# Unit-step transposes, a new order for the last stage's first two steps, and an earlier first load of h

## The chip, the cores and the metric

The kernel runs on one core of a Trainium2 chip. The metric is the device time of one execution in microseconds (us); before the change the median of three runs is 2382.28 us (2378.8 to 2383.4). The core has TensorE (PE in the profile, its weight loads PEld), VectorE (DVE), ScalarE (ACT), GpSimd (POOL), and SyncE (SP), whose queue issues nearly all DMA transfers. Each engine works through its own list of instructions in order and waits on semaphores of the others.

## The reference

A transformer block on 2048 tokens of width 1024, all in float32:

```python
xn = _layernorm(x)
q, k, v = split(xn @ wqkv)                 # 32 heads of 32
pq, pk = q @ w_phi, k @ w_phi              # per head
phi = concat(softmax(p), softmax(-p))      # per head, for q and for k: 64 features
kv, z = phi_k^T v, sum(phi_k)              # sums over all tokens
o = (phi_q kv) / (phi_q z + 1e-6)
s = o.reshape(S, D) @ wo
h = silu(xn @ w1) * (xn @ w3)              # 3584 wide
return x + s * silu(h @ w2)
```

## The kernel before

Every float32 product is made of three passes on split operands: `split(hi, lo, src)` writes a rounded copy on ScalarE (line 93) and the remainder on VectorE (line 94); TensorE then adds hi·hi, hi·lo and lo·hi. The large products are cut into 2 x 2 blocks and done as seven products with sums of blocks as operands. The seven operands of x are named A11, A12, S2, S1, S3, S4, A22 (`ANAMES`), those of the weights B11 to T4.

**Stage order.** The first stage computes h and stores it in HBM (`h_d`), with x's operands (`xo_d`) and the weights' operands prepared on the side. The second does keys and values, in two passes over eight pairs of token tiles, and then a third pass, the queries (`c == 2`): for each pair `i`, `seven` does seven products of twelve matmuls (line 679) into banks b, a, b, c, b, c, b. Bank b of a pair is one bank: A11's result is copied out of it by ScalarE (`k0`, line 798), then S2 is added into it, copied out (`d0`, line 811), and so on. The spikes (maximum, minimum, subtraction, exponential) follow on VectorE, GpSimd and ScalarE (lines 741 to 746) and go to HBM as `e_d`. The third stage is the product of h with w2 (line 1078), 56 steps of seven products; its operands come from `load_h`, `a_first` and `a_second`. The last stage applies the feature sums and the output projection.

**Loads of the queries.** `reload(i)` takes seven tiles of a ring of eleven (`quad`) and loads x's operands of the next pair at the start of each pair. h's first tile, of the same ring, is loaded by `load_h(0, 0)` in the middle of pair 6; `a_first(0, 0)` in pair 7 splits it.

**Who sets the order.** In the queries the lists of SP and TensorE are as written; those of ScalarE, VectorE and GpSimd are ordered by a planner that has costs for every instruction and fills an engine's idle time with work that it takes to be ready. In the last stage all five lists are as written (`in_order`).

**The last stage.** Tokens are taken in eight steps `b` of two tiles (`SETS[b]`). For a step:

- `load_e(b, c)` loads the exponentials `es` (SP); partition r of a group of 32 and the index u stand for token 4r + u.
- `weigh(b, c)` multiplies them by z, four instructions on GpSimd (line 1005); `add_up(b, c)` sums them per head, four on VectorE (line 1013); `factors(b)` makes the two factors of a head from the sums, seven on VectorE (lines 1022 to 1028); `weights(b)` scales es by them, two on VectorE and two on GpSimd (line 1035).
- `swap(b, c)` transposes blocks of 32 x 32, four instructions on VectorE (line 1042), into `ets`. It writes them so that tokens stand in their own order, 4r + u: each transposed row is written with a step of four floats.
- `heads_out(po)` multiplies with kv on TensorE (128 small matmuls, line 1052) into four banks `po`.
- `operand(t, po)` splits tile t's part of po into the operand `oT` of the projection (lines 93, 94 again).
- `half_out(oT, a, c)` is one projection product of 24 matmuls (line 1205) for tile a and output half c, into one of three banks (`pm`).
- `result(m, p)` multiplies product m with the gate on VectorE (line 1224), which frees the bank, adds x on GpSimd (line 1225), stores the output and loads the gate and x of product m + 3 into one of four `gx` buffers.

A step's TensorE work is: product 0, product 1, the head matmuls for the next step, product 2, product 3 (in step 0 the head matmuls stand behind product 2). Step 0 prepares steps 1 and 2, later steps a little further ahead.

Of the kernel before, what the change touches and what calls it, by code (L numbers as in the profile page):

```python
# [8 lines left out]
F = mybir.dt.float32  # L9
# [8 lines left out]
P = 128  # L18
# [10 lines left out]
def tile_kernel(ctx: ExitStack, tc: tile.TileContext, x, wkT, wqT, wv, wphi, wo, w1, w3, w2, out):  # L29
    nc = tc.nc  # L30
# [33 lines left out]
    ANAMES, BNAMES = [n for _, n, _ in ORDER], [n for _, _, n in ORDER]  # L64
# [26 lines left out]
    def split(hi, lo, src, by=None):  # L91

        nc.scalar.copy(hi, src)  # L93
        (by or nc.vector).tensor_sub(lo, src, hi.bitcast(F))  # L94
# [199 lines left out]
    for j in range(4):  # L294
        sl = slice(32 * j, 32 * j + 32)
# [260 lines left out]
    def operand(k, n):  # L556

        r = raw_of(k)
        src = {"B11": r["B11"], "B21": r["B21"], "T2": wk[4], "T1": r["B11"], "T3": r["B12"], "B22": r["B22"], "T4": r["B21"]}[n]
        bos[k, n] = quad("bo")  # L560
        split(bos[k, n][:, 0], bos[k, n][:, 1], src.rearrange("p (k n) -> p k n", n=P))
# [305 lines left out]
    def load_h(kb, i):  # L867
        hq = quad("hr", F)
        nc.sync.dma_start(hq.rearrange("p b k t -> p (b k t)"),
                          h_d[i // 4][kb][i % 4].rearrange("p b h k t -> p (b h k t)"))  # L870
        return hq
# [44 lines left out]
    for c in range(3):  # L916
        wbn = {}
        if c == 2:
            in_order(ENG.SP, ENG.PE)
            close("spare")  # L920
            bpa = pool("ra", 1, side="right")
        for i in range(len(pairs)):
            nxt, end = {}, i + 1 == len(pairs)

            def steps():
                for j in range(7):
                    if c == 0 and 4 <= 7 * i + j < 40:
                        split_wo(7 * i + j - 4)
                    if j == 0:
                        if i + 2 == len(pairs) and c < 2:  # L930
                            for m in range(2):
                                wbn.update(fetch(c + 3, m))
                        if not (end and c == 2):
                            nxt.update(reload((i + 1) % len(pairs)))
                        if c == 2 and i in (1, 2):
                            load_b(0, i - 1)
                    if c == 2 and end and j in (2, 3):
                        load_b(0, j)
                    for todo in (later, later_s):
                        if todo:  # L940
                            todo.pop(0)()

                    if end and c < 2:
                        if j < 4 or (j == 4 and c == 0):
                            wbn.update(fetch(c + 3, j + 2))
                        if j == 6 and c == 1:
                            wbn.update(fetch(c + 3, 6))
                    if c == 2 and (i, j) == (6, 4):
                        ahead[0, 0] = load_h(0, 0)
                    if c == 2 and (i, j) == (7, 1):  # L950
                        ready.append(a_first(0, 0))
                    if c == 2 and (i, j) == (7, 4):
                        ready.append(a_second(*ready[0]))
                    if c == 2 and (i, j) == (7, 5):
                        ahead[0, 1] = load_h(0, 1)
                    yield

            pend = (queries if c == 2 else heads)(i, xo, wb, steps(), pend)
            xo = nxt
        wb = wbn  # L960
# [38 lines left out]
    def weigh(b, c):  # L999

        z = zb[:, c].unsqueeze(1).to_broadcast([P, 2, 256])
        for t in range(2):
            for u in range(2):
                ez[b, t, c, u] = work.tile([P, 2, 256], F, name="ez", tag="w")
                nc.gpsimd.tensor_mul(ez[b, t, c, u], es[b, t, c][:, 2 * u:2 * u + 2], z)  # L1005

    def add_up(b, c):

        if c == 0:
            zs[b] = small.tile([P, 4, 2, 2, 8], F, name="zs", tag="sums")  # L1010
        for t in range(2):
            for u in range(2):
                nc.vector.tensor_reduce(zs[b][:, 2 * u:2 * u + 2, t, c], ez.pop((b, t, c, u)).rearrange("p u (h f) -> p u h f", f=DH),  # L1013
                                        axis=AX.X, op=OP.add)

    def factors(b):

        s4 = s_in[:, :, b // 4, b % 4].rearrange("p u (h s) -> p u h s", s=2)
        z4 = zs.pop(b).rearrange("p u t c (h s) -> p u (t c h) s", s=2)
        by[b] = work.tile([P, 4, 2, 2, 8], F, name="by", tag="h1", bufs=2)  # L1020
        b4 = by[b].rearrange("p u t c (h s) -> p u (t c h) s", s=2)
        nc.vector.reciprocal(rho, s4[:, :, :, 1])
        nc.vector.tensor_mul(rho, s4[:, :, :, 0], rho)
        nc.vector.tensor_mul(den, z4[:, :, :, 1], rho)
        nc.vector.tensor_add(den, z4[:, :, :, 0], den)
        nc.vector.reciprocal(b4[:, :, :, 0], den)
        nc.vector.tensor_mul(b4[:, :, :, 1], b4[:, :, :, 0], rho)
        nc.vector.tensor_copy(by0, by[b][:, :, :, 0])
# [8 lines left out]
    def swap(b, c):  # L1037

        for q in range(2):
            ets[c, q] = accp.tile([P, 4, 2, 32, 4], F, name="et", tag=f"acc{4 + 2 * c + q}")  # L1040
            for t in range(2):
                nc.vector.transpose(ets[c, q][:, :, t].rearrange("p k r u -> p u k r"),  # L1042
                                    es[b, t, c][:, :, 128 * q:128 * q + 128].rearrange("p u (k f) -> p u k f", f=DH))

    def heads_out(po):

        for c in range(2):
            for s in range(2):
                for j in range(4):
                    for a in range(4):  # L1050
                        sl = slice(32 * a, 32 * a + 32)
                        nc.tensor.matmul(po[a][32 * j:32 * j + 32, 256 * c:256 * c + 256], kvt[sl, c, j, s],  # L1052
                                         ets[c, j // 2][sl, 2 * (j % 2) + s].rearrange("p t r u -> p (t r u)"),
                                         start=c == 0 and s == 0, stop=c == 1 and s == 1, skip_group_check=True)

    def operand(t, po):

        two = [quad("oT") for _ in range(2)]
        for m, (a, src) in enumerate(po):
            o = two[a // 2].rearrange("p u (b c) t -> p u b c t", c=2)  # L1060
            if src.shape[1] == 2:
                split(o[:, 0], o[:, 1], src.rearrange("p b (c t) -> p b c t", c=2)[:, :, :, P * t:P * t + P])
            else:
                split(o[:, 0, a % 2], o[:, 1, a % 2], src.rearrange("p (c t) -> p c t", c=2)[:, :, P * t:P * t + P])
        return two

    def product(kb, i, bank, r, ao, b, an, bn):
# [162 lines left out]
    def weights(b):  # L1230

        scale(b, 0, nc.vector)
        scale(b, 1, nc.gpsimd)
# [7 lines left out]
    for b in range(NB):  # L1241
        p0 = half_out(oT, 0, 0)
        if b == 0:
            add_up(1, 1)
            factors(1)
            weights(1)
            swap(1, 0)
            load_e(3, 0)
            swap(1, 1)
            load_e(3, 1)  # L1250
            weigh(2, 0)
        else:
            result(4 * b - 1, last)
            if b + 1 < NB:
                swap(b + 1, 1)
                load_e(b + 3, 1)
            if b + 2 < NB:
                weigh(b + 2, 1)
                add_up(b + 2, 1)
                factors(b + 2)  # L1260
        p1 = half_out(oT, 0, 1)
        result(4 * b, p0)
        if 0 < b < NB - 1:
            heads_out([po[a // 2][:, a % 2] for a in range(4)])
        p2 = half_out(oT, 1, 0)
        result(4 * b + 1, p1)
        if b == 0:
            weigh(2, 1)
            add_up(2, 0)
            heads_out([po[a // 2][:, a % 2] for a in range(4)])  # L1270
            nxt = [operand(t, [(0, po[0]), (2, po[1])]) for t in range(2)]
            add_up(2, 1)
            factors(2)
            weights(2)
        else:
            if b + 2 < NB:
                weights(b + 2)
            if b + 1 < NB:
                nxt = [operand(t, [(0, po[0]), (2, po[1])]) for t in range(2)]
        if b + 2 < NB:  # L1280
            swap(b + 2, 0)
            load_e(b + 4, 0)
        if b + 3 < NB:
            weigh(b + 3, 0)
        last = half_out(oT, 1, 1)
        result(4 * b + 2, p2)
        if b + 3 < NB:
            add_up(b + 3, 0)
        oT = nxt
# [41 lines left out]
```

## Time and profile before

| what | value |
|---|---|
| median of three runs | 2382.28 us (2378.8 to 2383.4) |
| the profiled execution: time, span | 2379.08 us, 2377.0 us |
| granted TensorE clock, mean | 0.997 |
| busy, share of the span: DVE, ACT, POOL | 75%, 36%, 32% |
| queries (third pass) | about 1488 to 1635 us |
| product with w2 | about 1635 to 2172 us |
| last stage | about 2172 to 2377 us |

A row of the profile's timeline gives start, length, engine, line, operation, what it writes and reads with the shape, how many instructions of a kind are merged, and in brackets how long the engine stood idle before it and what ended that. Consecutive instructions overlap a little (the next starts before the last has drained), so the spacing from start to start is what an engine spends. A row of the waits gives engine, line and what it waited for: us in total, times, longest. A row by stretches of time gives span, busy time (and count) of PE, PEld, DVE, ACT, POOL, then the granted clock, the transfers' share and GB/s.

### The profile page before, as it was taken

The page shows a single profiled execution, that of the slowest core. Times are in us where ns is not written, and L with a number is a line of the kernel's source. Part 1 is how long each engine was busy: PE and PEld are TensorE (multiplying, and loading weights), DVE is VectorE, ACT ScalarE, POOL GpSimd, SP SyncE. Part 2 cuts the span into 40 slices and gives each one's busy share as a digit, 9 for nine tenths or more (in the row PEclk, how much of TensorE's full clock was granted, in tenths as well). Part 3 has the DMA queues.
Part 4 walks back from the last instruction along what each step waited for, and adds up shares of the span by engine and source line. Part 5 has one row for each costly group of instructions (what it writes and reads, how often), then busy time and mean ns, then how long its engine had stood idle before and what let it go on. Part 6 is the DMA issues. An engine that isn't in the chain of part 4 may idle for free. (4 is left out here: it accounts for less than half of the span.)

```text
span 2377.0 us, 35821 instructions
## 1 busy us (share of the span) xinstructions
PE 2341.7 (99%) x13298; PEld 1927.9 (81%) x13298; DVE 1771.6 (75%) x2511; ACT 856.9 (36%) x1506; POOL 758.4 (32%) x569
## 2 busy tenths in 40 slices
PE   6999999999999999999999999999999999999999
PEld 5888888888788888888888788887888888887777
DVE  8567798775688878885576665787678788888993
ACT  6445554443354444453221211234423222242010
POOL 1233555452455555652000000230011111114872
PEclk9999999999999999999999999999999999999999
DMA  7667789877877787776998867998444453277653
GB/s 263 198 217 235 233 288 315 285 251 224 258 272 263 247 280 274 262 270 224 362 347 337 321 221 281 348 352 294 154 145 158 177 185 138 94 274 293 222 190 121
DMA packets 319406, 586.83 MB, mean 247 GB/s; under 512 B 25600, under 2 KB 158208, under 8 KB 316544
## 3 DMA queue, kind: packets, MB, share of 16 engines
q1 hardware_dynamic: 304448, 569.87, 69.7%
q10 hardware_dynamic: 14784, 14.68, 1.8%
q8 instruction: 105, 1.72, 0.3%
q14 instruction: 69, 0.57, 0.1%
HBM read 379.19 MB, written 205.79 MB: 246 GB/s over the span
## 5 line engine op out<-in xcount | busy, mean ns | idle before, releaser
L94 DVE TENSOR_TENSOR bo<-rw,bo 128x512 fp32r<-128x512 f32 x336 | 310.7, 925 | 150.9 <-ACT bo L93 148.5
L1088 POOL TENSOR_TENSOR acc<-acc,u 128x512 f32<-128x512 f32 x48 | 63.5, 1323 | 450.9 <-ACT u L1087 427.9
L93 ACT CAST bo<-rw 128x512 fp32r<-128x512 f32 x336 | 201.1, 617 | 3.9 <-DMA w_d0T<-w2o 2.0
L1078 PE MATMUL bankb<-bo,as 128*128 128x512 f32 x816 | 200.7, 389 | 0.0
L1078 PEld LDWEIGHTS bankb<-bo,as 128*128 128x128 f32 x816 | 153.2, 188 | 31.8
L1205 PE MATMUL pm<-wos,oT 128*128 128x512 f32 x720 | 168.8, 393 | 3.6 <-DVE gx L1224 3.6
L627 PE MATMUL bankb<-op0A,bo 128*128 128x512 f32 x672 | 164.0, 391 | 0.3 <-DVE op0A L94 0.3
L1205 PEld LDWEIGHTS pm<-wos,oT 128*128 128x128 f32 x720 | 135.6, 189 | 35.1 <-DVE gx L1224 4.0
L627 PE MATMUL bankb<-op0S,bo 128*128 128x512 f32 x672 | 163.5, 392 | 0.0
L627 PE MATMUL bankc<-op0S,bo 128*128 128x512 f32 x672 | 163.0, 391 | 0.0
L627 PE MATMUL bankc<-op1S,bo 128*128 128x512 f32 x672 | 161.5, 389 | 0.9 <-ACT bo L93 0.9
L627 PE MATMUL bankb<-op1S,bo 128*128 128x512 f32 x672 | 161.6, 389 | 0.8 <-ACT h L569 0.8
L627 PE MATMUL bankb<-op1A,bo 128*128 128x512 f32 x672 | 161.4, 389 | 0.0
L627 PEld LDWEIGHTS bankc<-op1S,bo 128*128 128x128 f32 x672 | 126.0, 188 | 27.5 <-ACT bo L93 1.3
L627 PEld LDWEIGHTS bankb<-op1S,bo 128*128 128x128 f32 x672 | 126.0, 188 | 27.4 <-ACT h L569 1.2
L627 PEld LDWEIGHTS bankb<-op1A,bo 128*128 128x128 f32 x672 | 126.1, 188 | 26.2
L627 PEld LDWEIGHTS bankb<-op0A,bo 128*128 128x128 f32 x672 | 125.4, 188 | 25.9 <-DVE op0A L94 0.5
L627 PEld LDWEIGHTS bankb<-op0S,bo 128*128 128x128 f32 x672 | 125.6, 188 | 25.7
L627 PEld LDWEIGHTS bankc<-op0S,bo 128*128 128x128 f32 x672 | 125.5, 188 | 25.7
L1078 PE MATMUL bankc<-bo,as 128*128 128x512 f32 x576 | 146.2, 389 | 0.0
L1078 PEld LDWEIGHTS bankc<-bo,as 128*128 128x128 f32 x576 | 108.1, 188 | 22.5
L129 POOL TENSOR_TENSOR rw<-rw 128x512 f32<-128x512 f32 x56 | 82.8, 1479 | 135.5 <-DMA rw<-in_w 104.3
(246 smaller groups left out, 4726.1 us busy)
## 6 DMA issues: line engine op xcount, KB each, us to landing
rw<-in_w SPq DMA_DIRECT2D x224, 256.0 KB, 3.4
hr<-h_d SPq DMA_DIRECT2D x56, 512.0 KB, 4.1
xoS<-xo_d0S SPq DMA_DIRECT2D x48, 512.0 KB, 8.7
xoS<-xo_d1S SPq DMA_DIRECT2D x48, 512.0 KB, 7.1
xoA<-xo_d0A SPq DMA_DIRECT2D x36, 512.0 KB, 7.2
xoA<-xo_d1A SPq DMA_DIRECT2D x36, 512.0 KB, 6.1
e<-e_d SPq DMA_DIRECT2D x32, 512.0 KB, 6.2
h_d<-h SPq DMA_DIRECT2D x56, 256.0 KB, 3.9
```

What stands on the lines that cost most here:

```text
L93: nc.scalar.copy(hi, src)
L94: (by or nc.vector).tensor_sub(lo, src, hi.bitcast(F))
L129: nc.gpsimd.tensor_sub(b12, b22, b12)
L627: nc.tensor.matmul(bank, bt[:, w, kk], aos[tb][an][:, u, kk], start=an in ("A11", "A12", "S1") and n == 0, stop=LAST[b] == an and n == 11, ...
L1078: nc.tensor.matmul(bank[b], t[:, u, pos + k], bos[kb, bn, k][:, w], start=first and n == 0, stop=LAST[b] == an and n == 5, skip_group_chec ...
L1088: nc.gpsimd.tensor_add(c, c, u)
L1205: nc.tensor.matmul(p, oT[a][k // 4][:, u, k % 4], wos[c, 4 * (k % 2) + k // 2][:, w], start=n == 0, stop=n == 23)
```

## The change

It has four parts. `swap` writes a transposed row with steps of one float, so that the tokens stand in the order (u, r); `heads_out` keeps that order, and `operand` restores the tokens' order when it reads `po`, with one split for each of the two column halves instead of one for both. Step 0 of the last stage has its work in another order: the sums and weighings of step 2 move ahead of the first two results, the head matmuls come directly behind product 2, each operand is split by itself, the result of product 2 comes ahead of the second operand and of the transposes, and both swaps of step 2 are done in step 0. Step 1 starts with the weighing of step 3 and the result of product 3, and does its sums and factors behind the head matmuls. In the queries, `load_h(0, 0)` is issued after the third of the last seven loads of x's operands, at the start of pair 6, instead of in its middle.

```diff
@@ queries, inside steps() @@
-                        if not (end and c == 2):
+                        if c == 2 and i == 6:
+                            nxt.update(reload(7, ANAMES[:3]))
+                            ahead[0, 0] = load_h(0, 0)
+                            nxt.update(reload(7, ANAMES[3:]))
+                        elif not (end and c == 2):
                             nxt.update(reload((i + 1) % len(pairs)))
...
-                    if c == 2 and (i, j) == (6, 4):
-                        ahead[0, 0] = load_h(0, 0)
@@ swap @@
-            ets[c, q] = accp.tile([P, 4, 2, 32, 4], F, name="et", tag=f"acc{4 + 2 * c + q}")
+            ets[c, q] = accp.tile([P, 4, 2, 4, 32], F, name="et", tag=f"acc{4 + 2 * c + q}")
             for t in range(2):
-                nc.vector.transpose(ets[c, q][:, :, t].rearrange("p k r u -> p u k r"),
+                nc.vector.transpose(ets[c, q][:, :, t].rearrange("p k u r -> p u k r"),
@@ heads_out @@
-                                         ets[c, j // 2][sl, 2 * (j % 2) + s].rearrange("p t r u -> p (t r u)"),
+                                         ets[c, j // 2][sl, 2 * (j % 2) + s].rearrange("p t u r -> p (t u r)"),
@@ operand @@
-        for m, (a, src) in enumerate(po):
-            o = two[a // 2].rearrange("p u (b c) t -> p u b c t", c=2)
+        for a, src in po:
+            o = two[a // 2].rearrange("p v (b c) (r u) -> p v b c r u", c=2, u=4)
             if src.shape[1] == 2:
-                split(o[:, 0], o[:, 1], src.rearrange("p b (c t) -> p b c t", c=2)[:, :, :, P * t:P * t + P])
+                src = src.rearrange("p b (c t u r) -> p b c t r u", c=2, t=2, u=4)
+                for c in range(2):
+                    split(o[:, 0, :, c], o[:, 1, :, c], src[:, :, c, t])
             else:
-                split(o[:, 0, a % 2], o[:, 1, a % 2], src.rearrange("p (c t) -> p c t", c=2)[:, :, P * t:P * t + P])
+                src = src.rearrange("p (c t u r) -> p c t r u", c=2, t=2, u=4)
+                split(o[:, 0, a % 2], o[:, 1, a % 2], src[:, :, t])
@@ last stage, loop over b @@
             weigh(2, 0)
+            add_up(2, 0)
+            weigh(2, 1)
+        elif b == 1:
+            weigh(3, 1)
+            result(3, last)
         else:
             result(4 * b - 1, last)
...
         result(4 * b + 1, p1)
-        if b == 0:
-            weigh(2, 1)
-            add_up(2, 0)
-            heads_out([po[a // 2][:, a % 2] for a in range(4)])
-            nxt = [operand(t, [(0, po[0]), (2, po[1])]) for t in range(2)]
-            add_up(2, 1)
-            factors(2)
-            weights(2)
+        if b < 2:
+            if b == 0:
+                heads_out([po[a // 2][:, a % 2] for a in range(4)])
+            add_up(b + 2, 1)
+            nxt = [operand(0, [(0, po[0]), (2, po[1])])]
+            factors(b + 2)
+            weights(b + 2)
+            if b == 0:
+                result(2, p2)
+            nxt.append(operand(1, [(0, po[0]), (2, po[1])]))
...
         if b + 2 < NB:
-            swap(b + 2, 0)
-            load_e(b + 4, 0)
+            for c in range(2 if b == 0 else 1):
+                swap(b + 2, c)
+                load_e(b + 4, c)
...
         last = half_out(oT, 1, 1)
-        result(4 * b + 2, p2)
+        if b:
+            result(4 * b + 2, p2)
```

## The prediction

> **What bounds it.** Read first the busy shares, then TensorE's waits, then its timeline, then the other engines around each gap.
>
> ```profile
> PE 2341.7 (99%) x13298; PEld 1927.9 (81%) x13298; DVE 1771.6 (75%) x2511; ACT 856.9 (36%) x1506; POOL 758.4 (32%) x569
> ...
> PE pm L1205 <- DVE gx L1224: 3.6, 1, 3.6
> PE bankb L679 <- ACT k L798: 2.2, 1, 2.2
> PE bankb L1078 <- DVE acc L1090: 1.0, 1, 1.0
> ...
> 1614.11 2.88 PE L679 MATMUL banka<-op4B,xoA 128*128 128x512 f32 x12
> 1619.15 4.60 PE L679 MATMUL bankb<-op4T,xoS 128*128 128x512 f32 x12 [2.17 <-ACT k L798]
> 2188.87 2.75 PE L1052 MATMUL po<-et,kvt 32*32 32x256 f32 x128
> 2197.13 5.60 PE L1205 MATMUL pm<-wos,oT 128*128 128x512 f32 x24
> 2206.35 6.68 PE L1205 MATMUL pm<-wos,oT 128*128 128x512 f32 x21 [3.62 <-DVE gx L1224]
> ```
>
> TensorE is busy 99% of the span: other engines' time counts only where it makes TensorE wait. From the queries on there are two waits of over 1 us, and each costs more than its idle time. After 2.17 us idle, twelve matmuls took 4.60 us where the twelve before took 2.88: 1.72 more. After 3.62 us, 21 took 6.68 us; at the spacing of the row before (24 in 5.60, so about 0.227 each and 0.16 for the last to drain) they take 4.93: 1.75 more. So the wait at 1619 costs 3.89 us and the one at 2206 costs 5.37. Their sum, 9.26 us, is about all that reordering can win here.
>
> ```profile
> 1620.00:1640.00 20.00, 20.00 (x83) 16.35 (x82) 18.16 (x28) 7.96 (x12) 3.15 (x3) 0.92 0.99 346
> ```
>
> This row of 20 us holds the span, the busy time of five engines, the granted clock, and the transfers' share: the clock is 0.92 right behind the shorter gap, so its 1.72 us is a slowed clock. [...]
>
> **The first wait.** In the queries' seventh pair ScalarE, whose order the planner writes, reached h's first cast early and stood there:
>
> ```profile
> 1592.25 0.86 SPq L526 DMA_DIRECT2D xoS<-xo_d1S  x2
> 1595.26 3.04 SPq L526 DMA_DIRECT2D xoS<-xo_d1S  x2
> 1603.78 0.32 SPq L526 DMA_DIRECT2D xoA<-xo_d1A  x1
> 1604.19 0.38 SPq L869 DMA_DIRECT2D hr<-h_d  x1
> DMA to landing us min/median/max: 7.4/8.8/9.9
> ...
> 1595.17 1.06 ACT L746 ACTIVATE eq<-eq 128x1024 f32<-128x1024 f32 x1 [3.06 <-POOL eq L744]
> 1596.67 0.59 ACT L798 COPY k<-bankb 128x512 f32<-128x512 f32 x1 [0.44 <-ACT eq L746]
> 1600.71 0.59 ACT L811 COPY d<-bankb 128x512 f32<-128x512 f32 x1 [0.93 <-PE bankb L679]
> 1611.49 0.62 ACT L93 CAST af<-hr 128x512 fp32r<-128x512 f32 x1 [6.03 <-DMA hr<-h_d]
> 1617.57 1.06 ACT L746 ACTIVATE eq<-eq 128x1024 f32<-128x1024 f32 x1 [3.97 <-POOL eq L744]
> 1618.53 0.57 ACT L798 COPY k<-bankb 128x512 f32<-128x512 f32 x1
> ...
> 1612.15 0.69 DVE L94 TENSOR_TENSOR af<-hr,af 128x512 fp32r<-128x512 f32 x1 [3.33 <-ACT af L93]
> ```
>
> hr is issued at 1604.19, lands about 1611.5, and ScalarE (6.03 us) and VectorE (3.33 us) wait for it. Behind VectorE's stands d (L823), then its maxima, GpSimd's subtraction, the exponential at 1617.57, and behind that the copy of A11's bank, which frees the bank for S2 on TensorE.
>
> The change issues hr fourth of eight loads. That place is now the second of the pair at 1592.25, about 1592.7. Landing 8.8 us later (the xoS median, the row under the SP rows), hr is there at 1601.5, ten us sooner. SP does not change its count: S1, S3, S4 and A22 each move one place, to 1595.3, about 1598, 1603.8 and 1604.2. With the longest landing, 9.9, the last is there at 1614.1; none of the four is multiplied before 1619. The ring of eleven operand tiles hands out as many tiles, so hr's earlier hold costs nothing I can find.
>
> Unknown is where the planner now puts the cast. In this trace it stands where ScalarE was idle soon after the issue. If it stands behind the copy at 1600.71, hr has landed: the whole 3.89 us go. If between the copies of 1596.67 and 1600.71, ScalarE waits until 1601.5, casts twice (0.5 each), perhaps runs one exponential (1.0), and copies by 1603.1 to 1604.1; TensorE wants that bank at about 1603.4: 0 to 0.8 us lost. If ahead of 1596.67, see the second rival. I take the full 3.89, since each next wait (the copy then due at 1614.3 for S2 at 1617) has its work done.
>
> **The second wait, at 2206.** A product's bank (three of them) is freed by `result`; the second step's second product takes the first step's third bank, whose result stood last in VectorE's list:
>
> ```profile
> 2171.90 1.41 DVE L94 TENSOR_TENSOR oT<-po,oT 128x256 fp32r<-128x256 f32 x4
> 2175.27 0.56 DVE L1022 RECIPROCAL stat<-s_in 128x64 f32<-128x64 f32 x1
> 2177.76 2.35 DVE L1035 TENSOR_TENSOR e<-e,stat 128x1024 f32<-128x1024 f32 x2
> 2180.03 7.52 DVE L1042 STREAM_TRANSPOSE et<-e 128x512 f32<-128x512 f32 x8
> 2187.38 1.28 DVE L1224 TENSOR_TENSOR gx<-pm,gx 128x512 f32<-128x512 f32 x2
> 2188.57 2.46 DVE L1013 TENSOR_REDUCE zs<-ez 128x16 f32<-128x512 f32 x4
> 2192.25 2.63 DVE L94 TENSOR_TENSOR oT<-po,oT 128x512 fp32r<-128x512 f32 x4 [1.22 <-ACT oT L93]
> 2194.80 2.46 DVE L1013 TENSOR_REDUCE zs<-ez 128x16 f32<-128x512 f32 x4
> ...
> 2205.61 0.69 DVE L1224 TENSOR_TENSOR gx<-pm,gx 128x512 f32<-128x512 f32 x1
> ...
> 2181.35 5.07 POOL L1005 TENSOR_TENSOR ez<-e,zb 128x512 f32<-128x512 f32 x4
> 2188.20 2.52 POOL L1225 TENSOR_TENSOR gx<-gx 128x512 f32<-128x512 f32 x2 [1.78 <-issue]
> ```
>
> *Spacings.* From start to start: a transpose 0.92 (7.35 for 8), a reduction 0.62, factors 2.5, two scalings 2.27, a result 0.6, an oT subtraction 0.64 whole and 0.33 half.
>
> *Transposes.* They now write unit steps instead of every fourth float. Bounds: 0.92 (writing in shorter steps shouldn't lose) and 0.62, the reduction of equal size. *Operands.* The order of tokens is now restored where oT is read from PSUM, in steps of 32 floats, and the four whole pieces per step become eight halves on ScalarE and on VectorE. Bounds per half: 0.33, and 0.92, as if half a piece cost a whole stepped transpose. I take the transpose at 0.62 and charge the halves the same extra per element (0.30 over 512, so 0.15): 0.48. ScalarE's halves are covered: it is busy 2.25 us of a turn of 24.66 (the row under "Later turns").
>
> [...]
>
> *VectorE's list by these prices.* Eight first halves cost 8 x 0.15 = 1.2 more: factors start at 2176.5, scalings end 2181.2, eight transposes 2186.2 (the head matmuls want them at 2188.9). GpSimd's four weighings end 2187.7, so the moved sums end 2188.3 and two results 2189.5; the fourth product wants the first bank at 2191.6. GpSimd's next four, now ahead of its two result additions, end 2192.7 (so the first two results are stored about 2 us later, and the loads behind those stores on SP's queue too; their gx is used only by results after 2208). Sums 2193.3, first operand 2195.3 (wanted 2197.0), factors 2197.8, scalings 2200.0, and the third result at **2200.6, wanted at 2202.6**: the wait is gone with 2.0 to spare. Then second operand 2202.5, eight transposes 2207.5 (wanted 2208.0 and, for the second half, 2209.3), four sums 2210.0, fourth result 2210.6, wanted at 2210.7. That last is what is late next, with no margin: 0 to 0.5 us. With transposes still at 0.92 and halves at 0.33 the same list gives 2200.2 for the third result and 2211.9 for the fourth: 1.2 lost, 4.2 of 5.37 won.
>
> *Later turns.*
>
> ```profile
> 2241.06:2265.72 24.66, 24.66 (x225) 19.74 (x225) 23.39 (x39) 2.25 (x4) 18.88 (x14) 1.00 0.67 230
> ```
>
> A turn lasts 24.66 us, all TensorE. VectorE's spacings in it: 7.35 transposes, 4.9 sums, 2.5, 2.3, 2.55 oT, 2.4 results, 22.0 in all; after, 8 x 0.62 and 8 x 0.48 for the first and the fifth: 20.9. So the earlier start (5.4) is kept to the end; results, head matmuls and loads are as far ahead of need as now. The last product's tail is untouched.
>
> **Sum.** 3.89 + 5.37 = 9.3 off this execution: 2379.08 us (span 2377.0) to 2369.8. It lies 3.2 below the median of the three runs (2382.28, from 2378.8 to 2383.4), so the median goes to **2373.0**, 0.39% faster. A difference within 0.2% (4.8 us) is about what a measurement of this kernel can't tell from none.
>
> **Rivals.** *One: stepped PSUM reads make VectorE the bound, and it ends slower.* Place: the halves on L94. A turn without transposes and oT is 22.0 - 7.35 - 2.55 = 12.1; with transposes at 0.92 it fills TensorE's 24.66 when a half costs 0.65 us [(24.66 - 12.1 - 7.35)/8], with 0.62 when it costs 0.95 [(24.66 - 12.1 - 4.96)/8]. At 0.92 and unimproved transposes a turn is 12.1 + 7.35 + 7.36 = 26.8: 2.1 over, six turns, 13 us, and some 8 in the first two turns; less the 9.3: about 2394. For it: no row with such a read. Against: the 16-byte step of the transposes costs at most 0.30 on 512. Chance 0.06.
>
> *Two: the wait on hr moves instead of going.* The cast ahead of the copy at 1596.67: hr at 1601.5, two casts, an exponential and its store issue (1.4), the copy: 1604.6, where S2 starts now at 1597.9: 6.7 and 1.7 of clock, 8.4 against 3.9. Total 9.3 - 8.4 = 0.9 gained: 2381.4. For it: ScalarE idles 3.06 us before 1595.17 and took the cast early once. Against: the load would be under 3 us old there. With the wait merely kept as large as now, 2376.9. Chance of either 0.24.
>
> *Three: the last stage gives half or less* (unchanged transposes with halves over 0.5, so that the fourth result and the head matmuls wait), the first wait gone: 2376 to 2378.4. Chance 0.12. *Four: neither pays,* 2382: 0.06.
>
> **Chances and range.** Both waits gone 0.52, at 2372 to 2374.5. Rival two splits: half of its 0.24 ends just beyond 0.2%, half within. Rival three within for two thirds. Faster 0.52 + 0.12 + 0.04 = 0.68, same 0.24, slower 0.08. The range takes in the two cases above 2376 and, below, the lowest run minus all waits of the list, 2378.8 - 9.3 - 1.0 = 2368.5: 2368 to 2382. Own range of the likeliest: 2370 to 2376.
>
> **What would show it.** No wait of TensorE at L679 for ScalarE's k copy and a granted clock of 1.00 after 1600; no cast of hr waiting there. No gap at pm near 2206, and the third result near 2200. Transposes about 0.6 to 0.75 apart, oT subtractions x8 a turn at 0.4 to 0.5. Wrong would make it: a wait of the first casts in front of 1600, halves of 0.65 or more, or a new gap before the second step's third product, near 2211.

## The result, and the profile after

The changed kernel takes 2366.73 us (median of six runs, 2363.33 to 2367.77) against 2378.81 us for the kernel before (six runs, 2376.16 to 2383.4): a ratio of 0.9950 with a 95% interval of 0.9939 to 0.9962, so 0.5% faster. The forecast was 9.3 us less than a median of 2382.28, a ratio of 0.9961, and 2373.0 us with a range of 2368 to 2382. The direction and the two named waits were right; the size was too small and the time lies 1.3 us below the range. The reasons follow below.

The busy shares, from the changed kernel's page:

```profile
PE 2337.4 (99%) x13298; PEld 1925.0 (81%) x13298; DVE 1753.2 (74%) x2539; ACT 859.2 (36%) x1534; POOL 760.5 (32%) x569
```

All of its TensorE waits behind the start-up, from its list of waits (us in total, times, longest):

```profile
PE bankc L627 <- ACT bo L93: 1.0, 1, 1.0
PE pkv L665 <- DVE ev L711: 0.9, 1, 0.9
PE pkv L839 <- DVE zs L838: 0.8, 1, 0.8
PE bankc L679 <- ACT d L818: 0.3, 1, 0.3
```

All three waits that the prediction quoted are gone: ScalarE's copy (2.2 us), VectorE's addition in the product with w2 (1.0) and the result (3.6). None took their place.

**The queries.** Timeline row of TensorE in the changed kernel:

```profile
1616.58 2.88 PE L679 MATMUL bankb<-op4T,xoS 128*128 128x512 f32 x12
```

SP's timeline row of the load of h:

```profile
1592.46 0.39 SPq L869 DMA_DIRECT2D hr<-h_d  x1
```

ScalarE's timeline, the first cast of h and the copy of A11's bank:

```profile
1605.89 0.62 ACT L93 CAST af<-hr 128x512 fp32r<-128x512 f32 x1 [0.68 <-PE bankb L679]
1615.34 0.57 ACT L798 COPY k<-bankb 128x512 f32<-128x512 f32 x1
```

And the row by stretches (span, busy time of PE, PEld, DVE, ACT, POOL, then clock, transfers' share, GB/s):

```profile
1600.00:1640.00 40.00, 40.00 (x178) 33.09 (x177) 35.25 (x53) 16.80 (x24) 6.31 (x6) 1.00 0.92 312
```

S2 starts without a wait, takes the undisturbed 2.88 us, and the clock is 1.00 where it was 0.92. h is issued at 1592.46 (forecast 1592.7) and lands 10.3 us later, at about 1602.8 (forecast 8.8 us later, 1601.5). Its cast runs at 1605.89 and no longer waits for h but for TensorE: the cast writes into a tile of the same ring of eleven, and that tile is free only when a product that reads it ends. In ScalarE's list the cast stands where it stood before, behind the copy at line 818 (1604.88 before, 1604.63 now). The copy that held TensorE runs at 1615.34, 1.2 us ahead of S2.

**The last stage.** VectorE's timeline in the changed kernel:

```profile
2174.15 4.86 DVE L1044 STREAM_TRANSPOSE et<-e 128x512 f32<-128x512 f32 x8
2178.93 2.42 DVE L1015 TENSOR_REDUCE zs<-ez 128x16 f32<-128x512 f32 x4
...
2186.16 0.42 DVE L94 TENSOR_TENSOR oT<-po,oT 128x256 fp32r<-128x256 f32 x1
2187.02 0.76 DVE L94 TENSOR_TENSOR oT<-po,oT 128x256 fp32r<-128x256 f32 x2 [0.44 <-ACT oT L93]
2188.22 0.42 DVE L94 TENSOR_TENSOR oT<-po,oT 128x256 fp32r<-128x256 f32 x1 [0.44 <-ACT oT L93]
2188.56 0.55 DVE L1024 RECIPROCAL stat<-s_in 128x64 f32<-128x64 f32 x1
...
2193.31 0.68 DVE L1229 TENSOR_TENSOR gx<-pm,gx 128x512 f32<-128x512 f32 x1
...
2203.41 1.88 DVE L1229 TENSOR_TENSOR gx<-pm,gx 128x512 f32<-128x512 f32 x3
```

And TensorE's:

```profile
2182.99 2.76 PE L1054 MATMUL po<-et,kvt 32*32 32x256 f32 x128
...
2191.25 10.36 PE L1210 MATMUL pm<-wos,oT 128*128 128x512 f32 x45
...
2204.91 10.49 PE L1210 MATMUL pm<-wos,oT 128*128 128x512 f32 x45
```

Everything here lies 5.88 us earlier than before (head matmuls at 2182.99 for 2188.87). The third result starts at 2193.31 and, at 0.6 us for a result, is done at 2193.9; TensorE wants it at 2196.7, 24 matmuls behind 2191.25: 2.8 us to spare where there were 3.6 us of wait. The fourth, first of the three at 2203.41, is done at 2204.0, and the product that takes its bank starts at 2204.91. Eight transposes take 4.78 us from start to start (2174.15 to 2178.93), 0.60 each.

TensorE's start times at fixed points tell where the 11.1 us between the two profiled spans (2377.0 and 2365.9) came from:

| point | before | after | earlier by |
|---|---|---|---|
| A11 of the queries' pair 6 | 1592.35 | 1592.10 | 0.25 |
| first product with w2 | 1634.50 | 1630.17 | 4.33 |
| last bank a of that stage | 2158.03 | 2152.43 | 5.60 |
| first projection product | 2172.46 | 2166.58 | 5.88 |
| head matmuls of step 1 | 2213.64 | 2202.22 | 11.42 |

So the queries gave 4.1 us (3.9 forecast), the last stage 5.5 (5.4 forecast), and **the product with w2 gave 1.3, and the head matmuls at its end 0.3, that the sum did not hold**. The first 0.25 us were there before the change could act, and of the 11.4 at the last row the two spans keep 11.1.

### The profile page after: what moved, and what is told of

Same layout as the page of the kernel before. It is cut to its first block, busy times and chain, and to the rows that moved or that the text cites. A ratio compares the mean times of both kernels' runs of the same rounds, so it can differ in the third digit from the quotient of the medians.

```text
span 2365.9 us, 35878 instructions
## 1 busy us (share of the span) xinstructions
PE 2337.4 (99%) x13298; PEld 1925.0 (81%) x13298; DVE 1753.2 (74%) x2539; ACT 859.2 (36%) x1534; POOL 760.5 (32%) x569
## 3 DMA queue, kind: packets, MB, share of 16 engines
q8 instruction: 105, 1.72, 0.3%
## 4 chain that ended last, share of the span: by engine, by line
PE 95%; DMA 2%; DVE 2%; SPq 1%; issue 1%; ACT 0%; POOL 0%; ACTq 0%; POOLq 0%; DVEq 0%
PE bankb L627 25%; PE bankb L1083 13%; PE bankc L627 12%; PE bankb L679 11%; PE pm L1210 7%; PE bankc L1083 6%; PE banka L627 6%; PE bankc L679 5%; PE banka L1083 3%; PE banka L679 3%; PE po L1054 1%; PE pkv L665 1%; PE pw L248 1%; SPq L166 0%; PE pt L219 0%
## 5 line engine op out<-in xcount | busy, mean ns | idle before, releaser
L1095 DVE TENSOR_TENSOR acc<-bankb,acc 128x512 f32<-128x512 f32 x152 | 104.3, 686 | 30.8 <-PE bankb L1083 26.6
```

Source lines behind the costliest of these rows:

```text
L1095: nc.vector.tensor_add(c, pb, c)
```

## Experiments

The executions also differ in the first stage, which none of the edits touches: the last wait of the list above (ScalarE's d, early in the queries) ends anywhere from 1506.58 to 1511.12 us in the eleven profiles. So beside the times stands TensorE's time from that matmul's start to the start of the kernel's last three matmuls (on the tile `late`):

| kernel | us, from first to last | ratio of times to before (95%) |
|---|---|---|
| before | 861.13 | |
| changed | 850.01 | 0.9950 (0.9939 to 0.9962) |
| load alone | 857.96 | 0.9979 (0.9971 to 0.9988) |
| all but the load | 854.49 | 0.9973 (0.9963 to 0.9983) |
| layout alone | 865.12 | 0.9998 (0.9989 to 1.0007) |
| all but the layout | 852.82 | 0.9957 (0.9944 to 0.9971) |
| load sixth | 849.88 | 0.9955 (0.9940 to 0.9970) |
| first swap stepped | 850.91 | 0.9960 (0.9946 to 0.9975) |
| halves in turn | 850.03 | 0.9950 (0.9935 to 0.9965) |
| one result moved | 863.03 | 1.0006 (0.9997 to 1.0015) |
| one swap moved back | 851.87 | 0.9952 (0.9938 to 0.9965) |

The two rows of TensorE's timeline that bound it, in before:

```profile
1510.62 3.01 PE L679 MATMUL bankc<-op4B,xoS 128*128 128x512 f32 x12 [0.32 <-ACT d L818]
2371.75 0.84 PE L1205 MATMUL pm<-late,oT 128*128 128x512 f32 x3
```

And in the changed kernel:

```profile
1510.36 3.01 PE L679 MATMUL bankc<-op4B,xoS 128*128 128x512 f32 x12 [0.32 <-ACT d L818]
2360.37 0.84 PE L1210 MATMUL pm<-late,oT 128*128 128x512 f32 x3
```

### The load alone, and all but the load

The first is the kernel before with only this edit, the second the changed kernel without it:

```diff
-                        if not (end and c == 2):
+                        if c == 2 and i == 6:
+                            nxt.update(reload(7, ANAMES[:3]))
+                            ahead[0, 0] = load_h(0, 0)
+                            nxt.update(reload(7, ANAMES[3:]))
+                        elif not (end and c == 2):
...
-                    if c == 2 and (i, j) == (6, 4):
-                        ahead[0, 0] = load_h(0, 0)
```

> The kernel before with h's first load moved ahead of the last four operand loads, nothing else. Theory: each of three waits of TensorE has one cause of its own, and the load is that of the wait at 1619 only. Then 2.17 us of idle time and its slowed restart (1.72) are gone, about 4 us; the 1.0 us wait at 2156 and the 3.6 us wait at 2206 stay, with a 1.2 to 1.8 us slower restart behind the last: 4 us faster than before, 0.17%. Rival A (the load also moves the short wait in the product with w2, through the planner's order): 5.2 us, and no wait at L1078. Rival B (the wait on h only moves): a wait of TensorE on ScalarE near 1600 instead, and no gain.

> The changed kernel with h's first load back in the middle of pair 6. Theory: one wait of 2.2 us for ScalarE's copy near 1619 comes back with its slowed restart, so 4 us slower than the changed kernel and 7 to 8 us faster than before; all else as in the changed kernel. Rival A (the load also removed the short wait at 2156): 5.2 us slower than the changed kernel, with a wait at L1083 of 1 us.

Load alone: 2373.52 against 2377.90 us. All but the load: 2370.85. TensorE's timeline with the load alone, rows with a wait from the queries' middle on:

```profile
2151.20 1.65 PE L1080 MATMUL bankb<-late,as 128*128 128x512 f32 x6 [0.87 <-DVE acc L1092]
2200.92 7.69 PE L1207 MATMUL pm<-wos,oT 128*128 128x512 f32 x21 [3.62 <-DVE gx L1226]
```

The same with all but the load:

```profile
1617.12 4.43 PE L679 MATMUL bankb<-op4T,xoS 128*128 128x512 f32 x12 [2.60 <-ACT k L798]
```

With the load alone only the queries' wait is gone, and the other two stand as they did (0.87 and 3.62 us); without the load only that wait is back. The short wait at L1080 does not hang on the load, so rival A falls, and no wait of the first casts appears near 1600, so rival B falls. The 861.13 - 857.96 = 3.2 us of load alone are less than 3.9, and the restart behind the 3.62 us gap makes up for the rest: it cost 1.0 more in that execution (21 matmuls in 7.69 us, not 6.68).

### Load sixth instead of fourth

```diff
-                            nxt.update(reload(7, ANAMES[:3]))
+                            nxt.update(reload(7, ANAMES[:5]))
                             ahead[0, 0] = load_h(0, 0)
-                            nxt.update(reload(7, ANAMES[3:]))
+                            nxt.update(reload(7, ANAMES[5:]))
```

> The changed kernel with h's first load sixth of the eight, behind S3, instead of fourth. Theory: the cast of h cannot start before about 1605.9 whatever the load does, because its target is a tile of the same ring of eleven that TensorE reads until S3's product ends; so any load that has landed by then is as good. Sixth means an issue at about 1598 and a landing at 1605 to 1608: at most 2 us of wait on ScalarE for h and no wait of TensorE, same time as the changed kernel. Rival D (the load's place alone decides, each us later in landing is lost): 2 to 4 us slower with TensorE waiting for the copy near 1617.

No wait of TensorE behind 1520, and 849.88 us by the table: the changed kernel to within 0.2. SP's timeline:

```profile
1594.98 0.32 SPq L869 DMA_DIRECT2D hr<-h_d  x1
```

ScalarE's:

```profile
1603.15 0.62 ACT L93 CAST af<-hr 128x512 fp32r<-128x512 f32 x1 [0.67 <-PE bankb L679]
```

In this execution the queries run 2.75 us earlier, so this issue is 5.3 us later than the changed kernel's in relation to them. The cast starts at the same place to 0.01 us (1605.89 - 2.75 = 1603.14) and again waits for TensorE, not for h. What sets the cast is the ring tile that it writes; the load need only have landed by then. Rival D falls.

### Layout alone, and all but the layout

"Layout" is `swap`, `heads_out` and `operand` of the changed kernel; the first kernel puts them into the kernel before, the second takes them out of the changed one.

```diff
-                nc.vector.transpose(ets[c, q][:, :, t].rearrange("p k r u -> p u k r"),
+                nc.vector.transpose(ets[c, q][:, :, t].rearrange("p k u r -> p u k r"),
...
+                for c in range(2):
+                    split(o[:, 0, :, c], o[:, 1, :, c], src[:, :, c, t])
```

> The kernel before with unit-step transposes and the operands split by halves, its old order and load. Theory: the transposes go from 0.92 to 0.60 apart, which takes away the 1.0 us wait at 2156 (VectorE's sums in the product with w2 come sooner), but not the one at 2206: VectorE cannot split the operands before the head matmuls end at about 2191.6, and behind that point the eight halves at 0.60 (with their waits on ScalarE) cost 2.2 more than four pieces did, sums, factors and scalings cost the same, and four transposes save 1.3; the third result ends at about 2206.6 against 2206.3. So about 1 us faster than before, 0.05%. Rival C (the shorter transposes alone remove the wait at 2206, twelve of them ahead of the third result saving 0.32 each, 3.8 us against a wait of 3.6): 6 us faster than before.

> The changed kernel with the old transposes (step of four) and whole operand pieces; the new order and the moved load stay. Theory: the third result comes at about 2200 by the written order alone, so the wait at 2206 is gone; the next late one is the fourth result, behind eight transposes at 0.92: 0 to 1.5 us of wait before the second step's third product; the 1.0 us wait at 2156 is back. So 2 to 3 us slower than the changed kernel and 8 us faster than before. Rival C (the transposes were what removed the wait): 5 us or more slower than the changed kernel, with a gap of over 2 us at pm.

Layout alone: 2377.46 against 2377.90 us, no difference that can be told. All but the layout: 2368.00. TensorE's timeline, rows with a wait from the queries' middle on, layout alone:

```profile
1619.97 3.01 PE L679 MATMUL bankb<-op4T,xoS 128*128 128x512 f32 x12 [2.43 <-ACT k L798]
1641.12 1.65 PE L1081 MATMUL bankb<-bo,as 128*128 128x512 f32 x6 [0.18 <-ACT acc L1087]
1649.01 2.93 PE L1081 MATMUL bankb<-bo,as 128*128 128x512 f32 x6 [2.14 <-DVE acc L1093]
2209.65 7.84 PE L1208 MATMUL pm<-wos,oT 128*128 128x512 f32 x21 [4.33 <-DVE gx L1227]
```

All but the layout:

```profile
2151.91 1.66 PE L1080 MATMUL bankb<-late,as 128*128 128x512 f32 x6 [1.70 <-DVE acc L1092]
2206.75 10.45 PE L1207 MATMUL pm<-wos,oT 128*128 128x512 f32 x45 [0.75 <-DVE gx L1226]
```

VectorE's first half of an operand in step 0, layout alone:

```profile
2194.61 0.42 DVE L94 TENSOR_TENSOR oT<-po,oT 128x256 fp32r<-128x256 f32 x1 [3.60 <-ACT oT L93]
```

With the layout alone the wait for the result is not shorter but longer, 4.33 for 3.62 us. Eight of the saved transposes lie ahead of the head matmuls' end, which VectorE must wait for anyway: it stands idle 3.60 us ahead of the first half, where it stood 1.22 before. Behind that point the eight halves take 4.8 us from start to start (0.60 each, as in the changed kernel from 2186.16 to 2188.56) where the four whole pieces took 2.55, and the last four transposes save only 1.3. Rival C falls. The short wait in the product with w2 (2156 before) is gone. The 2.14 us at 1649 were not expected; in that execution a store of the exponentials was issued late on ScalarE (at 1645.99, where the exponential ended at 1643.58), with casts and VectorE's addition behind it (idle 2.35 us on ScalarE ahead of the first cast, 2.18 on VectorE). It was seen in one profile, whose 2383.61 us lie above that kernel's median, and why the store was late stays open.

Without the layout the order alone removes the 3.6 us wait; the fourth result is then late by 0.75 us (0 to 1.5 expected) and the wait in the product with w2 is back. Of the 852.82 - 850.01 = 2.8 us that the layout is worth beside the other parts, these two waits are 2.45.

### The first swap with the old step

```diff
+            old = b == 0
...
-                nc.vector.transpose(ets[c, q][:, :, t].rearrange("p k u r -> p u k r"),
+                nc.vector.transpose(ets[c, q][:, :, t].rearrange("p k r u -> p u k r" if old else "p k u r -> p u k r"),
...
```

The operands that are split from this swap's head matmuls read `po` in its old order with it.

> The changed kernel with the old transposes (step of four) in the first swap alone, whose eight instructions stand in the product with w2; every later transpose keeps unit steps. Theory: the first swap's 8 x 0.32 us on VectorE are what brought the last additions there, the gates, the loads of the exponentials and the first sums forward, and so removed the 1.0 us wait at 2156: that wait is back, 1 to 1.3 us slower than the changed kernel, and nothing else moves. Rival E (the wait went with the planner's order or the load, or is chance): no wait of TensorE at L1083 and the same time.

TensorE's timeline, its only row with a wait behind 1520:

```profile
2152.36 1.65 PE L1084 MATMUL bankb<-late,as 128*128 128x512 f32 x6 [0.83 <-DVE acc L1096]
```

The wait is back, 0.83 us, and the only one; 850.91 by the table, 0.9 above the changed kernel. From the first product with w2 to the stage's last bank a TensorE takes 523.40 us here, 522.26 in the changed kernel and 523.53 before: of the 1.3 us in the product with w2, 1.1 came from eight transposes there. The 0.3 us at the head matmuls did not: those 128 take 3.39 us before, 3.11 in the changed kernel and 2.89 here, with the wait back. Their cause stays open. The way it went is seen in the timelines of ScalarE, SP, GpSimd and VectorE, before:

```profile
2145.28 1.06 ACT L988 ACTIVATE acc<-acc 128x1024 f32<-128x1024 f32 x1 [1.40 <-DVE acc L1090]
2146.78 2.75 SPq L996 DMA_DIRECT2D e<-e_d  x2
2152.61 5.04 POOL L1005 TENSOR_TENSOR ez<-e,zb 128x512 f32<-128x512 f32 x4 [3.08 <-DVE acc L1090]
2155.19 0.69 DVE L1013 TENSOR_REDUCE zs<-ez 128x16 f32<-128x512 f32 x1 [0.56 <-POOL ez L1005]
```

The same four in the changed kernel:

```profile
2139.76 1.06 ACT L990 ACTIVATE acc<-acc 128x1024 f32<-128x1024 f32 x1 [1.15 <-DVE acc L1095]
2141.26 2.75 SPq L998 DMA_DIRECT2D e<-e_d  x2
2146.92 5.04 POOL L1007 TENSOR_TENSOR ez<-e,zb 128x512 f32<-128x512 f32 x4 [2.90 <-DMA e<-e_d]
2149.49 0.69 DVE L1015 TENSOR_REDUCE zs<-ez 128x16 f32<-128x512 f32 x1 [0.57 <-POOL ez L1007]
```

All four come 5.5 to 5.7 us earlier while TensorE's stage came 4.33 earlier: an addition on VectorE behind fewer microseconds of transposes, then the gate, its store, the load of the exponentials in SP's list behind that store, GpSimd's product, and VectorE's sums, behind which TensorE's bank addition stood. Rival E falls.

### Halves in turn

```diff
+        if po[0][1].shape[1] == 2:
+            for c in range(2):
+                for a, src in po:
...
+                    split(o[:, 0, :, c], o[:, 1, :, c], src[:, :, c, t])
```

> The changed kernel with the halves of an operand taken in turn from the two bank pairs of po instead of both halves of one pair first. Theory: a half costs VectorE 0.34 us, stepped or not, and the 0.60 us that it takes in the changed kernel is waiting, since ScalarE's next read of the same pair of banks is held until VectorE has read it; alternating lets the two engines work on different pairs, so four halves take 1.4 to 1.8 us instead of 2.4. No change of time, as TensorE waits for none of it. Rival F (the stepped read itself is slow and the waits follow from it): still 0.55 to 0.6 us from one half to the next.

Before, four contiguous halves took 1.41 us at the opening of the last stage (the row at 2171.90 that the prediction quotes). VectorE's timeline in the changed kernel at the same place, stepped:

```profile
2166.03 1.41 DVE L94 TENSOR_TENSOR oT<-po,oT 128x256 fp32r<-128x256 f32 x4
```

VectorE's timeline in this kernel, in step 0:

```profile
2182.44 1.62 DVE L94 TENSOR_TENSOR oT<-po,oT 128x256 fp32r<-128x256 f32 x4
```

Stepped or not, four halves take 1.41 us where they come from four banks of their own; in turn they take 1.62 in a step, and 1.54 to the start of what follows, where the changed kernel needs 2.4 (2186.16 to 2188.56). So the stepped read shows no cost of its own here, and the rest was the two engines waiting for each other at the same banks: VectorE twice 0.44 us for ScalarE in the changed kernel's rows, and ScalarE 0.49 and 0.55 us for VectorE ahead of those casts (2186.62 and 2187.81 in its timeline). In this kernel VectorE shows no such wait and ScalarE 0.22 and 0.16 us. Rival F falls. The time (850.03) is that of the changed kernel: TensorE waits for none of it.

### One result moved, and one swap moved back

The first is the kernel before with the result of product 2 ahead of the transposes; the second the changed kernel with swap(2, 1) in step 1.

```diff
             weights(2)
+            result(2, p2)
...
-        result(4 * b + 2, p2)
+        if b:
+            result(4 * b + 2, p2)
```

> The kernel before with one move: in step 0 of the last stage the result of product 2 stands behind the scalings and ahead of the transposes, as in the changed kernel; transposes, operands, all other order and the load as before. Theory: the third result then ends at about 2202.6 and the wait at 2206 is gone, but TensorE, 5.4 us earlier, finds the next late work: the head matmuls of step 1 want swap(2, 1) at about 2209.3, which stands in step 1 behind the sums of step 3 (held by GpSimd to about 2210.5) and the fourth result and ends near 2214.8: a wait of 4 to 5.5 us at the head matmuls. Time within 2 us of before. Rival G (the place of that one result was the whole wait): 4 to 5.5 us faster than before, no gap behind 2200.

```diff
             result(3, last)
+            swap(2, 1)
+            load_e(4, 1)
...
-            for c in range(2 if b == 0 else 1):
-                swap(b + 2, c)
-                load_e(b + 4, c)
+            swap(b + 2, 0)
+            load_e(b + 4, 0)
```

> The changed kernel with swap(2, 1) and its load moved back into step 1, behind the fourth result. Theory: with transposes 0.60 apart swap(2, 1) then ends about 2.4 us behind the fourth result, near 2204.9, where the head matmuls of step 1 want its last tiles at about 2203.9: a wait of 0.5 to 1.5 us at the head matmuls, and the changed kernel's time plus that. Rival H (doing both swaps in step 0 is what removes the wait): 4 us or more slower than the changed kernel.

TensorE's timeline with the result moved:

```profile
1616.75 3.01 PE L679 MATMUL bankb<-op4T,xoS 128*128 128x512 f32 x12 [2.21 <-ACT k L798]
...
2210.53 1.11 PE L1052 MATMUL po<-et,kvt 32*32 32x256 f32 x16 [3.27 <-DVE et L1042]
2212.39 2.25 PE L1052 MATMUL po<-et,kvt 32*32 32x256 f32 x48 [0.75 <-DVE et L1042]
```

With the swap moved back:

```profile
2204.61 1.36 PE L1054 MATMUL po<-et,kvt 32*32 32x256 f32 x48 [0.52 <-DVE et L1044]
```

Moving the one result gains nothing (2380.28 against 2378.05 us): the wait turns up some 7 us further on, 3.27 and 0.75 us at the head matmuls, which want the second swap. Rival G falls: the result was the first late thing, the swap behind it the second. With the rest of the change in place, the swap's own place matters less. From the start of step 1's head matmuls to the product behind them TensorE takes 4.08 us with the swap moved back and 2.69 in the changed kernel: 1.4 us, of which 0.52 shows as a wait. The table's 1.9 has 0.45 more from the product with w2, where the two kernels do the same. Four us or more were rival H's, so it falls too. That the place matters less because the four transposes now take 2.4 us and not 3.7 is likely, but no run has this place with the old transposes and the rest of the change.

## Why the prediction was right and wrong

*The queries' wait* (forecast 3.89, measured 4.1): right in place, cause and size. Its open question, where the planner puts the cast, had an answer that the prediction missed: the planner left the cast where it was, and the cast's own target is a ring tile which TensorE holds until S3 ends, so it could not stand ahead of the two copies. Rival two, given 0.24, was excluded by that. The load took 10.3 us to land and not 8.8; 3.1 us ahead of the cast, that cost nothing.

*The last stage* (5.37, measured 5.5): right. The third result was forecast 2.0 us ahead of need and came 2.8 ahead. The fourth, called late next with no margin, had 0.9 us; with all but the layout it is late next indeed, by 0.75.

*The prices.* Transposes: 0.62 taken, 0.60 measured. Halves: 0.48 taken for a stepped read, 0.60 measured in the steps; the size was near by luck, since the stepped read takes 1.41 us for four as the contiguous one does (0.34 from 2188.22 to 2188.56, the last half in the changed kernel's rows) and the rest is waiting between the two engines that read the same banks; the argument for 0.48, an extra per element like the transposes', was wrong. Rival one, VectorE as the bound, needed 0.95 per half. Eight transposes took 7.35 us from start to start when they wrote with a step of 16 bytes in SBUF, and 4.78 with unit steps; a step of 128 bytes in PSUM, read by VectorE, showed no penalty (1.41 us for four halves with and without it).

*The step that failed: the transposes were costed in the last stage alone.* The first swap, eight transposes in the product with w2, was not followed. Its 8 x 0.32 us there let go of the 1.0 us wait at 2156, which the prediction quoted and took into the low end of its range alone; the sum put it at nothing. Missing from the sum were 1.3 us in that stage, 1.1 of them shown to be the transposes', and 0.3 at the head matmuls behind it, whose cause is open. With both it is 10.9, and the two profiled executions stand 11.1 apart.

*The other failed step: the reference point of the range.* The sum was put onto the median of three runs, 2382.28; over six it was 2378.81, and 2377.90 in the 24 of the next comparison. As a ratio the forecast of 0.9961 lies inside the measured interval, at its edge; as a time it was 3.5 us too high from that alone. Those 3.5 and the 2.8 us by which the sum was short (12.1 for 9.3) are the 6.3 us between 2373.0 and 2366.73; on the median of six the same sum gives 2369.5, inside the range. The low end, the lowest of three runs minus the sum and the 1.0 us wait, was no bound: with three more runs the lowest was 2376.16 and not 2378.8, and the eleven profiled executions spread over 4.5 us before they reach anything that was edited. That the measured difference of medians (12.1) is a little more than what the traces show (11.1) is within the interval and stays unresolved.

## What to carry to other kernels

When an instruction gets cheaper, list every place where it runs, and follow each to what waits behind it, through other engines' lists and queues if need be: a stage in which its engine is far from busy can still hold a wait that hangs on it. When a wait is removed, run the lists on to the next late thing before counting the gain; moving the one late result alone gained nothing here, because the next was 7 us behind. And a load moved earlier pays only up to the point where its consumer's other conditions (here a tile of the same ring: issued 5.3 us later, the load had its cast at the same place to 0.01 us) are met, so a look at those tells how early is enough.

## What the runs showed of the hardware that was not expected

Restarting TensorE behind a gap of about the same length cost very different amounts. By the rows above, against the undisturbed 2.88 us for twelve matmuls, 1.52 for six and 4.93 for 21 (the last the prediction's estimate, from 24 in 5.60): 2.17 us of idle time cost 1.72 more, 2.60 cost 1.55 and 2.14 cost 1.41 in the six behind it, but 2.21 and 2.43 cost only 0.13 each; 3.62 cost 1.75 in one execution and 2.76 in another, and 4.33 cost 2.91. So the price of a wait here was its idle time and anything from 0.1 to 2.9 us. The granted clock goes with it: from 1600 to 1640 it was 0.96 before (0.60 from 1620 to 1624) and 0.96 with all but the load, where the restart was slow, but 1.00 with the layout alone, where 2.43 us cost 0.13. What sets the clock behind a gap, and so the price, no run here shows.
